# Six of sixteen token tiles transposed by VectorE through DRAM instead of by TensorE

## The chip, the cores and the metric

The kernel runs on one core of one Trainium2 chip. The metric is the time of one execution on the device in microseconds (us). Before the change three runs took 562.86, 564.63 and 564.69 us, so the median is 564.63 us.

## The reference

The input `x` is 2048 tokens of 512 features in float32. It is normalised once, and two branches use the result: a linear attention with 32 heads of 16 features, and a gated feed-forward network with 1376 hidden features. Their outputs are multiplied and added to `x`:

```python
xn = layernorm(x)                                  # no scale, no shift, eps 1e-5
q, k, v = split(xn @ wqkv)                         # 32 heads of 16
pq, pk = q @ w_phi, k @ w_phi                      # per head, 16x16
phi_q = concat(softmax(pq), softmax(-pq))
phi_k = concat(softmax(pk), softmax(-pk))
kv, z = phi_k^T @ v, sum(phi_k)
s = ((phi_q @ kv) / (phi_q @ z + 1e-6)) @ wo
g = silu((relu(xn @ W_gate) * (xn @ W_up)) @ W_down)
out = x + s * g
```

## The kernel before, in words

**Precision.** Each float32 operand of a large matmul is split into a rounded high part and the low remainder (`split`, L193: ScalarE writes the high part, VectorE or GpSimd subtracts to get the low part). `mm3` (L198) then makes three matmuls of each product.

**Tiles and stages.** The 2048 tokens are 16 tiles of 128 tokens, in four blocks of four tiles. `order` (L219) alternates between two blocks: tiles 0 to 7 take turns between blocks 2 and 3, tiles 8 to 15 between blocks 0 and 1. So tiles 2m and 2m+1 lie at the same place of two blocks.

Stage one is the loop over n at L1046, one token tile a turn. TensorE (PE in the profile) makes `pk` and `pv`, the key and value projections of tile n (12 matmuls each), and `pq`, a piece of the query projection (`query`, L364, 12 matmuls), and adds `pkv`, the key-value products of an earlier tile (`kv_products`, 8 matmuls). `query(n-1)` reads the transposed tiles of a group of four: in turn 9 `query(8)` reads tiles 8 to 11, and in turn 13 `query(12)` reads tiles 12 to 15. The vector engines make the softmax features of `pk` (`exponents`, `features`). GpSimd (POOL) splits the features and issues a DMA that adds them into the sum `zacc` (`features_split`, L429).

Stage two, from about 167 us, goes twice over 11 slices of the hidden features (`gate_up`, `down`), half of the tokens each time. It uses a 2x2 block product with seven products in place of eight, so the sums and differences S1 to S4 of the transposed tokens are wanted too. Beside it the queries' features are made on VectorE, ScalarE and GpSimd (`all_queries`, L1172). Each half ends with the output tiles (`pso`).

**The transposed tokens.** `XT` (L255) holds, for each token column, eight pieces in high and low parts: A21, A22 of the odd tile, A11, A12 of the even one, and S1 to S4. For tile m these steps make it:

- `load_x(m)`: a DMA from `x` on the queue of SyncE (SP).
- `norm_stats`, `norm_scale`, `norm_apply` (L259 to L276): ScalarE (ACT) makes mean and variance with two passes whose written output is not used (they go to the buffer `xn`), VectorE (DVE) and GpSimd make the scale, and ScalarE writes the normalised tile into `xn`.
- `turn(m)` (L320): four PE transposes of 128x128 into one PSUM bank `pxT`; ScalarE copies it to the high part of `XT` (`hi_xt`) and again to a full-precision buffer `xf` (`full_xt`); VectorE writes the low part (`lo_xt`) from `pxT`.
- `sums_x(m)` for odd m: GpSimd makes S1 to S4 from the two `xf` tiles with four operations into two new buffers `sa` and `sb`; `sums_hi` and `sums_lo` split them into `XT`.

In turn n the loop loads tile n+7, scales tile n+5, applies the norm to tile n+4, transposes tile n+3 between `pk` and `pv` (LEAD is 3, L30), and makes the statistics of tile n+6.

**What sets the order.** The program is written out by a planner, `Clock` (L62). Every engine runs its instructions in program order, and work that isn't urgent (weight preparation `f_prep`, the queries, the stores) is written as generators. `pump` lets a generator go on when the planner's estimate of the engines' time says that its inputs are ready; a DMA counts as landed 8000 PE cycles after its issue, with a margin of 3000 more before another step may use it. A generator that yields a number waits that many times 512 PE cycles. `finish` runs a generator to its end at once.

**Buffers.** Tiles of a tag share slots: 41 of 2 KB a partition (`u2`), 8 of 4 KB (`u4`: the features `ek`, the value parts `vhl`, raw weights), 8 PSUM banks of which `pkv` holds four through stage one. A new tile waits until an old one of its tag is let go.

Of the kernel before, what the change touches and what calls it, by code (L numbers as in the profile page):

```python
# [1 line left out]

# [11 lines left out]
P = 128  # L14
# [15 lines left out]
LEAD = 3  # L30
QUERIES = [(0, 1, 2), (6, 7, 4, 5, 3)]
# [10 lines left out]
A21, A22, A11, A12, S1, S2, S3, S4 = range(8)  # L42
# [19 lines left out]
class Clock:  # L62
# [7 lines left out]
    shared = None  # L70
# [13 lines left out]
    def issued(self, key, name, a, k):  # L84
        o, ins = a[0], [*a[1:], *k.values()]
        n = max(x.free_size() for x in [o, *ins] if hasattr(x, "free_size"))
        start = max([self.now, *(self.there(x) + 200 for x in ins)])
        if name == "dma_start":
            self.ready[o.name] = start + self.LANDING
            if key == "gpsimd":  # L90
                self.free[key] = max(start, self.free[key]) + self.ISSUE
            return
        cost = self.RATE[key] * n
        if key == "tensor":
            n = o.free_size()
# [6 lines left out]
        self.ready[o.name] = self.free[key] + (380 if key == "tensor" else 0)  # L102

# [55 lines left out]
def layer_kernel(ctx: ExitStack, tc: tile.TileContext, x, wkT, wqT, wv, wo, wf, cst, out):  # L159
# [15 lines left out]
    def u2(shape, name, dt=F32):  # L175
        return sb.tile(list(shape), dt, tag="u2", bufs=B2, name=name)
# [7 lines left out]
    def f32(t):  # L184
        return t.bitcast(F32)
# [68 lines left out]
    mhalf = sb.tile([P, 96], F32, name="mhalf")[:, 0:1]  # L254
    XT = sb.tile([P, 8, 2, 2, BT], F32R, tag="XT", name="XT")  # L255
    pace.shared = XT.name
    XN, XF, SF = {}, {}, {}

    def norm_stats(n):  # L259
        xt = X.pop(n)  # L260
        xn = u2((P, D), "xn")
        sm, ss, rs, bias = small(1, "lm"), small(1, "lv"), small(1, "lr"), small(1, "lb")
        nc.scalar.activation(xn, xt, AF.Copy, scale=-1.0 / D, accum_out=sm)
        nc.scalar.activation(xn, xt, AF.Square, bias=sm, accum_out=ss)
        XN[n] = xn, xt, bias, rs, sm, ss

    def norm_scale(n):
        xn, xt, bias, rs, sm, ss = XN[n]
        nc.vector.tensor_scalar(rs, ss, 1.0 / D, 1e-5, op0=ALU.mult, op1=ALU.add)
        nc.gpsimd.tensor_tensor(rs, rs, mhalf, op=ALU.pow)  # L270

    def norm_apply(n):
        xn, xt, bias, rs, sm, ss = XN[n]
        nc.vector.tensor_scalar(bias, sm, rs, None, op0=ALU.mult)
        nc.scalar.activation(xn, xt, AF.Identity, bias=bias, scale=rs)
        XN[n] = xn  # L276
# [32 lines left out]

    def hi_xt(n, p):  # L310
        nc.scalar.activation(xt_part(n, 0), p, AF.Copy)
# [5 lines left out]
    def lo_xt(n, p):  # L317
        add(nc.vector, xt_part(n, 1), p, f32(xt_part(n, 0)), ALU.subtract)
# [8 lines left out]
    def sums_x(n):  # L327

        x0, x1 = XF.pop(n - 1), XF.pop(n)
        sa, sb_ = u2((P, 2, 2, P), "sa"), u2((P, 2, 2, P), "sb")  # L330
        add(nc.gpsimd, sa[:, 0], x1[:, 0], x1[:, 1])
        add(nc.gpsimd, sb_[:, 0], x0[:, 0], x1[:, 0], ALU.subtract)
        add(nc.gpsimd, sa[:, 1], sa[:, 0], x0[:, 0], ALU.subtract)
        add(nc.gpsimd, sb_[:, 1], x0[:, 1], sa[:, 1], ALU.subtract)
        SF[n] = sa, sb_

    def sums_hi(n):
        for s, c in zip(SF[n], (S1, S3)):
            nc.scalar.activation(XT[:, c:c + 2, 0, :, cols(n)], s, AF.Copy)

    def sums_lo(n):
        for s, c in zip(SF.pop(n), (S1, S3)):
            add(nc.gpsimd, XT[:, c:c + 2, 1, :, cols(n)], s, f32(XT[:, c:c + 2, 0, :, cols(n)]), ALU.subtract)
# [112 lines left out]
    def f_load(f):  # L456
        if f == AHEAD[-1]:

            t = u4((P, 2, 2, 2, P), "rawg")
            RAW[f] = [t[:, c] for c in range(2)], u2((P, D), "rawd")  # L460
            nc.sync.dma_start(t.rearrange("p c k s f -> p (c k s f)"), wf[f][:, :1024])
        else:
            RAW[f] = two("rawg", f not in AHEAD), u2((P, D), "rawd")
            for c in range(2):
                nc.sync.dma_start(RAW[f][0][c].rearrange("p k s f -> p (k s f)"), wf[f][:, c * 512:(c + 1) * 512])
        nc.sync.dma_start(RAW[f][1], wf[f][:, 1024:])
# [520 lines left out]
    nc.sync.dma_start(wq_raw[:, 2:4, :], wqT[:, 2:4, :])  # L987
# [39 lines left out]

    def all_preps():
# [16 lines left out]
    at = [0]  # L1045
    for n in range(N):  # L1046
        at[0] = n
        if n + 7 < N:
            load_x(n + 7)
        if n == 2:  # L1050
            preps = pace.add(all_preps(), 0, 3)
        if 1 < n < N - 4:
            norm_apply(n + 4)
        if 0 < n < N - 5:
            norm_scale(n + 5)
# [5 lines left out]
        turned = [turn(n + LEAD)] if 1 < n < N - LEAD else [turn(3)] if n == 1 else []  # L1061
# [271 lines left out]
```

## Time and profile before

| What | Value |
|---|---|
| median of three runs | 564.63 us |
| the profiled execution, its time | 562.9 us |
| its span, first to last instruction | 561.1 us |
| PE busy | 556.3 us, 99% |
| DVE, ACT, POOL busy | 412.0, 282.7, 416.2 us |
| granted PE clock | 0.999 |
| DMA moved | 137.98 MB, mean 246 GB/s |
| PE transposes | 64, between 6.0 and 129.1 us |

The span is 1.8 us shorter than the execution's time. A row of the groups gives the engine, the operation, the output and inputs by name, their shape, the count, the busy time and mean duration, and the idle time that the engine spent just before these instructions. Matmul durations overlap (each is pipelined into the next), so the pace of PE is read from start to start, or from the pieces of the chain, which stand end to end. Nearly every instruction is issued through one helper, so line numbers say L58 throughout and the tiles' names tell the operations apart.

### The profile page before, as it was taken

Reading aid. Unit: us, or ns where it says so; the run is one execution under the profiler, and the core shown is the slowest. Engines: PE = TensorE matmul, PEld = TensorE weight load, DVE = VectorE, ACT = ScalarE, POOL = GpSimd, SP = SyncE. Lnnn points to the kernel's source line nnn. Section 1 sums busy time; section 2 is a strip of 40 time slices with the busy share of each in tenths; the row PEclk is TensorE's granted clock in tenths of the full one; section 3 lists DMA queues with packets and bytes.
Section 4 is the critical chain, followed back from the end, with each engine's and each line's share of the span. In section 5 each row is a group of like instructions: output and inputs, shape, how many; then the busy total and the mean of one; then the engine's idle time right before and its main releaser. Section 6 shows DMA issues by size and latency. Waiting matters only on the chain.

```text
span 561.1 us, 8204 instructions
## 1 busy us (share of the span) xinstructions
PE 556.3 (99%) x2618; PEld 466.0 (83%) x2618; DVE 412.0 (73%) x623; ACT 282.7 (50%) x504; POOL 416.2 (74%) x356
## 2 busy tenths in 40 slices
PE   9999999999999999999999999999999999999997
PEld 8888888888888888888888888888888888888886
DVE  5978777677656898999798432699995959775324
ACT  3898687765545456444425251234463544534500
POOL 1689987898888386998889242572879788888474
PEclk9999999999999999999999999999999999999999
DMA  8349999765599827979767899997475666659675
GB/s 282 136 150 245 274 277 330 213 167 166 150 297 314 327 77 276 326 270 324 263 240 230 246 356 419 401 374 282 137 225 178 219 204 206 207 166 284 170 237 193
DMA packets 84538, 137.98 MB, mean 246 GB/s; under 512 B 7824, under 2 KB 34320, under 8 KB 83600
## 3 DMA queue, kind: packets, MB, share of 16 engines
q1 hardware_dynamic: 81040, 125.33, 65.1%
q0 software_dynamic: 3312, 12.06, 11.0%
q8 instruction: 21, 0.34, 0.3%
q14 instruction: 21, 0.17, 0.1%
q10 hardware_dynamic: 144, 0.07, 0.0%
HBM read 76.87 MB, written 52.69 MB: 231 GB/s over the span
## 4 chain that ended last, share of the span: by engine, by line
PE 99%; DVE 0%; issue 0%
PE py L58 21%; PE pc L58 11%; PE pa L58 11%; PE pd L58 11%; PE pv L58 8%; PE pk L58 8%; PE pq L58 8%; PE pso L58 8%; PE pb L58 5%; PE pkv L58 3%; PE pnum L58 3%; PE pxT L58 1%; PE pfold L58 1%; PE pidle L58 1%; PE pz L58 0%; DVE yk L58 0%
## 5 line engine op out<-in xcount | busy, mean ns | idle before, releaser
L58 PE MATMUL py<-fdh,hl 128*128 128x512 f32 x176 | 68.5, 389 | 0.0
L58 PE MATMUL py<-fdh,hh 128*128 128x512 f32 x176 | 68.5, 389 | 0.0
L58 PE MATMUL py<-fdl,hh 128*128 128x512 f32 x176 | 68.5, 389 | 0.0
L58 PE MATMUL pa<-XT,wa 128*128 128x512 f32 x264 | 67.4, 389 | 0.0
L58 POOL TENSOR_TENSOR hl<-e,hh 128x512 fp32r<-128x512 f32 x22 | 28.5, 1296 | 44.9 <-ACT hh L58 40.0
L58 PEld LDWEIGHTS pa<-XT,wa 128*128 128x128 f32 x264 | 49.5, 188 | 10.2
L58 ACT ACTIVATE hh<-e 128x512 fp32r<-128x512 f32 x22 | 13.9, 633 | 72.5 <-DVE e L58 70.1
L58 DVE TENSOR_TENSOR y<-py,y 128x512 f32<-128x512 f32 x40 | 27.5, 689 | 24.7 <-PE py L58 24.7
L58 POOL TENSOR_TENSOR phl<-ek,phl 128x1024 fp32r<-128x1024 f32 x15 | 36.1, 2409 | 11.1 <-ACT phl L58 11.1
L58 PE MATMUL pv<-wvh,XT 128*128 128x512 f32 x128 | 43.5, 401 | 0.0
L58 PE MATMUL pk<-wkh,XT 128*128 128x512 f32 x128 | 42.4, 392 | 0.0
L58 POOL TENSOR_TENSOR hl<-u,hh 128x512 fp32r<-128x512 f32 x22 | 28.8, 1311 | 16.6 <-ACT hh L58 14.3
L58 POOL TENSOR_TENSOR ez<-eq,zB 128x1024 f32<-128x1024 f32 x16 | 38.5, 2411 | 3.3 <-ACT eq L58 2.7
L58 PE MATMUL pq<-XT,wqh 128*128 128x512 f32 (+1 forms) x144 | 40.3, 366 | 0.0
L58 PEld LDWEIGHTS py<-fdh,hl 128*128 128x128 f32 x176 | 33.0, 188 | 6.9
L58 PEld LDWEIGHTS py<-fdh,hh 128*128 128x128 f32 x176 | 33.0, 188 | 6.8
L58 PEld LDWEIGHTS py<-fdl,hh 128*128 128x128 f32 x176 | 33.0, 188 | 6.8
L58 POOL TENSOR_TENSOR ol<-of,oh 128x512 fp32r<-128x512 f32 (+1 forms) x13 | 19.9, 1551 | 23.3 <-ACT oh L58 15.9
L58 PE MATMUL pc<-XT,wc 128*128 128x512 f32 x132 | 34.9, 392 | 0.0
L58 PE MATMUL pd<-XT,wc 128*128 128x512 f32 x132 | 33.8, 389 | 0.0
L58 PE MATMUL pc<-XT,wb 128*128 128x512 f32 x132 | 33.7, 389 | 0.0
L58 PE MATMUL pd<-XT,wd 128*128 128x512 f32 x132 | 33.5, 389 | 0.0
(162 smaller groups left out, 1581.0 us busy)
## 6 DMA issues: line engine op xcount, KB each, us to landing
zacc<-ek POOLq DMA_DIRECT2D x15, 512.0 KB, 6.0
xts<-XT SPq DMA_DIRECT2D x4, 1792.0 KB, 8.8
XT<-xts SPq DMA_DIRECT2D x7, 1024.0 KB, 19.6
wa<-ws SPq DMA_DIRECT2D x26, 256.0 KB, 5.0
wb<-ws SPq DMA_DIRECT2D x26, 256.0 KB, 4.4
wc<-ws SPq DMA_DIRECT2D x26, 256.0 KB, 5.0
ws<-wa SPq DMA_DIRECT2D x22, 256.0 KB, 4.5
ws<-wb SPq DMA_DIRECT2D x22, 256.0 KB, 4.2
```

Source lines behind the costliest of these rows:

```text
L58: return self.tc.keep_in_program_order(op(*a, **k))
```

## The change: what it does

Tiles 10 to 15 (`BLOCKWISE = 10` and up) no longer go through `turn`. For them:

- `norm_stats` writes its unused outputs to a PSUM bank (`unread`); `xn` is taken later, in `norm_apply`, which writes the tile with the features in an order `(a k i)` in place of `(k a i)`, where i counts 32 features, a four groups and k four chunks.
- A generator `by_blocks` stores `xn` to DRAM (256 KB), waits, loads it back with four DMAs of 64 KB, one for each group of 32 partitions, so that 32-token pieces stand in the rows where they belong, and then lets VectorE transpose 32x32 blocks, 128x512 in one instruction. Its output `xf` is in the SBUF, with the tokens' blocks of 32 as an own axis. `hi_xt`, `lo_xt` and `sums_x` read it there; `full_xt` falls away.
- The main loop makes sure at the end of odd turns n that tiles n+1 and n+2 are done.

For all tiles, `sums_x` now writes its four results in the place of `xf` instead of into `sa` and `sb`; the order of S1 and S3 in `XT` is changed so that each pair written together lies together. Other parts: from turn 5 on tile n+8 is loaded, from turn 6 on statistics are made for n+7, from 7 on the scale for n+6, from 8 on the norm is applied to n+5. The last two pieces of `wq` and the gate/up weights of slice 3 are loaded with two DMAs in place of one. The queries of the first half no longer pause for 24 times 512 PE cycles after `state`.

```diff
+BLOCKWISE = 10
+LAND = (12, 12)
-A21, A22, A11, A12, S1, S2, S3, S4 = range(8)
+A21, A22, A11, A12, S3, S1, S2, S4 = range(8)
...
     def norm_stats(n):
         xt = X.pop(n)
-        xn = u2((P, D), "xn")
+        xn = None if n >= BLOCKWISE else u2((P, D), "xn")
+        unread = xn or ps(name="unread")
...
     def norm_apply(n):
+        xn = xn or u2((P, D), "xn")
+        if n < BLOCKWISE:
+            nc.scalar.activation(xn, xt, AF.Identity, bias=bias, scale=rs)
+            XN[n] = xn
+        else:
+            nc.scalar.activation(xn.rearrange("p (a k i) -> p k a i", a=4, i=32),
+                                 xt.rearrange("p (k a i) -> p k a i", a=4, i=32), AF.Identity, bias=bias, scale=rs)
+            TURN[n] = pace.add(by_blocks(n, xn), 0, 3, True)
+
+    def by_blocks(n, xn):
+        xd = dram((P, D), f"xn{n}")
+        yield "sync", xn
+        nc.sync.dma_start(xd, xn)
+        yield LAND[0],
+        yield "sync", xd
+        t = u2((P, 4, P), "xp")
+        for a in range(4):
+            r = slice(32 * a, 32 * a + 32)
+            nc.sync.dma_start(t[r], xd.rearrange("(b q) (a c) -> a q b c", q=32, a=4)[a])
+        yield LAND[1],
+        yield "sync", t
+        while at[0] < n - LEAD:
+            yield 1,
+        yield "vector", t
+        o = u2((P, D), "xf")
+        nc.vector.transpose(o, t.rearrange("p b c -> p (b c)"))
+        XF[n] = o.rearrange("p (b c k q) -> p c k b q", b=4, c=2, k=2)
+        yield "scalar", o
+        hi_xt(n, XF[n])
+        yield "vector", pace.mark("scalar")
+        lo_xt(n, XF[n])
+        if n % 2:
+            yield "gpsimd", o
+            sums_x(n)
...
     def sums_x(n):
         x0, x1 = XF.pop(n - 1), XF.pop(n)
-        sa, sb_ = u2((P, 2, 2, P), "sa"), u2((P, 2, 2, P), "sb")
-        add(nc.gpsimd, sa[:, 0], x1[:, 0], x1[:, 1])
-        add(nc.gpsimd, sb_[:, 0], x0[:, 0], x1[:, 0], ALU.subtract)
-        add(nc.gpsimd, sa[:, 1], sa[:, 0], x0[:, 0], ALU.subtract)
-        add(nc.gpsimd, sb_[:, 1], x0[:, 1], sa[:, 1], ALU.subtract)
-        SF[n] = sa, sb_
+        add(nc.gpsimd, x1[:, 1], x1[:, 0], x1[:, 1])
+        add(nc.gpsimd, x1[:, 0], x0[:, 0], x1[:, 0], ALU.subtract)
+        add(nc.gpsimd, x0[:, 0], x1[:, 1], x0[:, 0], ALU.subtract)
+        add(nc.gpsimd, x0[:, 1], x0[:, 1], x0[:, 0], ALU.subtract)
+        SF[n] = x1, x0
...
     for n in range(N):
         at[0] = n
-        if n + 7 < N:
-            load_x(n + 7)
+        up_to(n + 7 + (n > 4), load_x)
...
+        if n > 1:
+            up_to(n + 4 + (n > 7), norm_apply)
+        if n:
+            up_to(n + 5 + (n > 6), norm_scale)
...
-        turned = [turn(n + LEAD)] if 1 < n < N - LEAD else [turn(3)] if n == 1 else []
+        m = n + LEAD
+        if 1 < n < N - LEAD and m >= BLOCKWISE:
+            turned = []
+        else:
+            turned = [turn(m)] if 1 < n < N - LEAD else [turn(3)] if n == 1 else []
...
-        if n + 6 < N:
-            norm_stats(n + 6)
+        up_to(n + 6 + (n > 5), norm_stats)
         if n % 2 and n + 2 < N:
+            for m in (n + 1, n + 2):
+                if m in TURN:
+                    pace.finish(TURN.pop(m))
             sums_hi(n + 2)
...
             yield from state()
-            yield 24,
```

`up_to(m, op)` calls `op` for every tile up to m that hasn't had it.

More of the change, by code (lines that the diff above doesn't have):

```diff
@@ L1 @@
 from contextlib import ExitStack
+from types import SimpleNamespace
 import concourse.bass as bass
@@ L456, in f_load @@
     def f_load(f):
[L457 to L465, printed above, removed]
+        RAW[f] = two("rawg", f not in AHEAD), u2((P, D), "rawd")
+        for c in range(2):
+            nc.sync.dma_start(RAW[f][0][c].rearrange("p k s f -> p (k s f)"), wf[f][:, c * 512:(c + 1) * 512])
         nc.sync.dma_start(RAW[f][1], wf[f][:, 1024:])
```

52 lines of the change are left out of this document (30 added, 22 removed).

## The prediction

> **What bounds the kernel now.** I read the page's busy shares first, then the chain that ended last, then PE's own waits, and then the chain piece by piece around the turns that change.
>
> ```profile
> PE 556.3 (99%) x2618; PEld 466.0 (83%) x2618; DVE 412.0 (73%) x623; ACT 282.7 (50%) x504; POOL 416.2 (74%) x356
> ...
> PEclk9999999999999999999999999999999999999999
> ...
> PE 99%; DVE 0%; issue 0%
> ...
> PE pidle L58 <- DVE mhalf L58: 1.1, 1, 1.1
> ```
>
> The chain is PE from end to end, its only wait in the whole span is 1.1 us at the start, and its clock is full throughout. So only what PE executes, and any new wait of PE, moves the end. In the pieces of the chain (start, length, what) the turns stand one behind the other:
>
> ```profile
> 78.19 2.75 PE pk L58 x12
> 80.94 0.44 PE pxT L58 x4
> ...
> 87.81 2.75 PE pk L58 x12
> ...
> 97.44 2.75 PE pk L58 x12
> ...
> 103.38 2.72 PE pq L58 x12
> 106.10 2.72 PE pk L58 x12
> ...
> 115.69 2.72 PE pk L58 x12
> ...
> 125.27 2.72 PE pk L58 x12
> ...
> 134.86 2.72 PE pk L58 x12
> ...
> 144.00 2.72 PE pk L58 x12
> ```
>
> Each `pk` begins a turn. Turns 7 and 8 take 9.62 and 9.63 us, turn 9 takes 8.66 (it has no `pkv`), turns 10 to 12 take 9.59, 9.58 and 9.59. Turn 13, the first with no transposes, takes 9.14.
>
> **PE: what is removed.** Tiles 10 to 15 were transposed in turns 7 to 12: 24 of 64 transposes go. By difference: turns 7 and 8 save 0.48 and 0.49 against 9.14; turn 9 saves 0.50 against its three projections (3 x 2.72 = 8.16); turns 10 to 12 save 0.45, 0.44 and 0.45. The sum is 2.8 us. The lower bound is the six `pxT` pieces alone, 6 x 0.44 = 2.6; the upper is 6 x 0.50 = 3.0. I take 2.8, as it holds the handover to `pv` too.
>
> ```profile
> L58 PE MATMUL pxT<-ident,xn 128*128 128x128 f32 x64 | 9.9, 282 | 0.0
> ...
> L58 DVE STREAM_TRANSPOSE ez<-eq 128x512 f32<-128x512 f32 x16 | 10.7, 691 | 0.0
> ...
> L58 ACT ACTIVATE xf<-pxT 128x512 f32<-128x512 f32 x16 | 9.4, 588 | 0.0
> ...
> L58 DVE TENSOR_TENSOR XT<-pxT,XT 128x512 fp32r<-128x512 f32 x16 | 11.0, 690 | 6.9 <-ACT xf L58 5.4 <-ACT XT L58 1.5
> ...
> L58 DVE TENSOR_TENSOR yk<-yk,sx 128x512 f32<-128x512 f32 x1 | 1.3, 1254 | 0.0
> ...
> L58 POOL TENSOR_TENSOR sa<-xf 128x256 f32<-128x256 f32 x8 | 7.4, 926 | 0.2 <-ACT xf L58 0.2
> ```
>
> The 282 ns in the first row is not the price of a transpose: four take 0.44 us in the chain, 0.11 each. The Trainium skill (VectorE: DVE Perf Modes, The three transpose paths and Rules for kernel authors) says to use TensorE for a 128x128 transpose if PSUM will do as its destination, and puts one at 390 ns; by that figure 24 would save about 9.4 us, an estimate from that page, and the time would be near 555. By that figure the trace disagrees: its 0.11 us holds. Its advice against leaving TensorE has no cost in this trace either, since DVE is not in the chain.
>
> **DVE.** Six transposes of 128x512 are added: 6 x 0.69 = 4.1 us. Six low parts now have two SBUF inputs in place of PSUM and SBUF: between 0.69 and 1.25 each (the `yk` row, the nearest with two SBUF inputs), at most 3.4 more. Both lie beside PE as long as DVE has room:
>
> ```profile
> core 0: us, PE busy (x) PEld busy (x) DVE busy (x) ACT busy (x) POOL busy (x), PEclk, DMA share, GB/s
> ...
> 78.00:88.00 10.00, 10.00 (x52) 8.45 (x51) 7.47 (x12) 6.72 (x14) 9.74 (x11) 1.00 1.11 325
> 88.00:97.50 9.50, 9.50 (x49) 7.98 (x48) 8.22 (x14) 7.33 (x15) 6.58 (x6) 1.00 1.08 318
> 97.50:106.00 8.50, 8.50 (x41) 7.02 (x40) 5.59 (x10) 6.04 (x13) 8.42 (x12) 1.00 0.83 214
> 106.00:115.70 9.70, 9.70 (x50) 8.26 (x49) 6.42 (x12) 8.79 (x17) 8.07 (x9) 1.00 0.51 165
> 115.70:125.30 9.60, 9.60 (x49) 8.16 (x49) 8.04 (x12) 5.49 (x9) 9.52 (x10) 1.00 0.74 202
> 125.30:134.90 9.60, 9.60 (x49) 8.15 (x49) 6.73 (x10) 5.40 (x10) 9.12 (x9) 1.00 0.80 209
> ```
>
> DVE is idle at least 1.3 us in each stretch, a tile adds at most 1.25: zero on the path. Without that cover DVE's 4.1 to 7.5 us would be late for `pk`'s and `pv`'s readers.
>
> **ACT.** Six `xf` copies of 0.59 go, 3.5 us less. The high parts read SBUF instead of PSUM and the norm writes in pieces of 32; I cost both at nothing, between the same passes' present price and 0.1 us more each, as ACT is idle 0.9 us or more in every stretch above. The two statistics passes write to a PSUM bank: it takes a bank at turns 4 to 8, three turns or more before the one that `pxT` no longer takes. Turns 4 to 6 so want one bank more each (turn 6 two). Bounds: 0 to 0.6 us of PE in each of three turns (one pass of ACT before a bank is let go); I take 0, since PE waits for no bank now.
>
> **POOL.** The same four sums a pair, 0.93 us for the one shown, written in place; they now wait for DVE's transpose where they waited for `xf`. Nothing is added. Two buffers a pair are let go earlier.
>
> **SP and the DMA queues.** Six stores and 24 loads are added: 30 issues at some 0.33 us.
>
> ```profile
> 81.64 0.80 ACT L58 ACTIVATE xn<-xt,lb,lr 128x512 f32<-128x512 f32 x1
> ...
> L58 SPq DMA_DIRECT2D xt<-x x16: 327/352/7489, 0.7 to 85.7; - x16
> L58 ACT ACTIVATE xn<-xt x12: 615/631/667, 21.0 to 108.3; 128x512 f32<-128x512 f32 x12
> ...
> DMA to landing us min/median/max: 2.8/7.3/10.7
> ...
> ws<-wa SPq DMA_DIRECT2D x22, 256.0 KB, 4.5
> ...
> SPq L58 <- ACT pqs L58: 36.4, 10, 7.3
> ```
>
> These are a row of the timeline, three of the tile `xt` (durations are min/median/max in ns, then the first and last start), one of the DMA view and one of SP's waits. 30 x 0.33 is 10 us of SP spread over seven turns, while SP waits 36.4 us for `pqs` alone. Behind a load that waits for its store stand the next `xt` loads, the query spills and the weight stores. The `xt` load issued last, at 85.7, is read at 108.3, so it can be late by some 12 us. All of that costs 0.
>
> The tightest place is tile 11, which `query(8)` reads in turn 9. Its norm ends at 82.4. The planner counts 542 cycles for a matmul that takes 2.72 / 12 = 0.227 us in the chain, so its 3000 cycles before the store are 1.3 us (83.7), and the 12 x 512 + 8000 + 3000 between store and loads 7.2 us (90.9, or later if the store hasn't landed). With a landing of 7.3 us each, the median of `xt` (same size, same turns), the data is there at 98.3, and transpose, high and low part (0.69 + 0.6 + 0.7 to 1.25) end at 100.3 to 100.9. `query(8)` starts at 103.4 less two turns' saving, 102.4: 1.5 us or more to spare. Bounds: at 4.5 us (the `ws` row) the planner's second 7.2 us holds the transpose to 98.1, and 1.7 us are to spare; at 10.7 twice it is late by 5.3. I take 0.
>
> **The other edits.** The split of the `wq` and slice-3 loads adds two issues; PE waits for neither now: 0 (bounds -0.4 to 0.4, an issue each way). Loading, statistics and norms one tile earlier move ACT and SP work by a turn: 0. The new order of S1 to S4 moves addresses only: 0. Dropping the pause of 24 starts the first half's queries some 5 us sooner.
>
> ```profile
> 182.00:196.00 14.00, 14.00 (x63) 11.59 (x63) 11.76 (x19) 5.83 (x15) 5.97 (x4) 1.00 0.89 335
> 196.00:210.00 14.00, 14.00 (x64) 11.59 (x63) 13.83 (x20) 7.43 (x14) 11.12 (x11) 1.00 0.21 79
> ```
>
> DVE is full from 196 (13.83 of 14) and PE has no wait even then. Earlier by 5 us fills 182 to 196, where 2.2 us of DVE are free: 0, bounds 0 to 3 us (5 less the 2.2 free), taken at the cover that the rows show.
>
> **The sum.** 2.8 us less PE, all else beside it. The profiled execution took 562.9 us, 1.7 under the median of the runs shown; it would take 560.1. On the median, 564.63 - 2.8 = 561.8 us.
>
> **The rivals.**
>
> *Slower: the DMA engines fall behind, and features wait for buffers.* By 103 us the change adds both transfers of tiles 10 and 11 and the stores of 12 and 13: 6 x 0.262 = 1.57 MB, where the DMA share is already 0.83 to 1.11 from 78 on.
>
> ```profile
> 85.91 0.60 ACT L58 ACTIVATE vhl<-pv 128x512 fp32r<-128x512 f32 x1 [1.98 <-DMA zacc<-ek]
> ...
> 94.00 0.60 ACT L58 ACTIVATE vhl<-pv 128x512 fp32r<-128x512 f32 x1 [0.51 <-DMA zacc<-ek]
> ...
> 102.78 0.69 DVE L58 TENSOR_TENSOR ek<-pk,mx 128x512 f32<-128x512 f32 x1 [1.26 <-DMA zacc<-ek]
> ```
>
> For: buffers of the features are let go by the `zacc` DMA, and three times an engine already waits for it. At 320 GB/s the added bytes are 4.9 us of backlog. `pk` of turn 9 is let go at 104.1 (the row at 102.78 and one more subtraction), the next `pk` starts at 106.1: 2.0 us to spare. If each of the three waits grew by the backlog, PE would lose 3 x 2.9 = 8.7 us: 570.5. It decides when more than 5.6 us reaches PE. Against: `zacc` has a queue of its own, and turns without `pxT` hold a bank less. Chance 0.19.
>
> *Tile 11 is late.* The DMA view of 40 to 75 us has
>
> ```profile
> xt<-x SPq DMA_DIRECT2D x4, 256.0 KB, 10.2
> ```
>
> At 10.2 us for both landings the tile would be ready at 106.4 and PE would wait 4.0 at `query(8)`: 565.8; at the bound of 5.3, 567.1. It decides from a landing of some 8 us twice. Against: the median of 7.3. Chance 0.16.
>
> *The change doesn't do what it says: POOL holds the turn.* POOL is busy 9.52 of 9.60 in turn 11 and 9.12 in turn 12, so a turn of 9.14 leaves it no room. If each of the six new low parts shuts POOL out for its 1.25 us, POOL loses 7.5 us; two of them fall before 97.5, where it is idle 3.2 us from 78 on, and four (5.0 us) between 97.5 and 134.9, where it is idle 2.3. The 2.7 us left over would pass to PE and eat the gain: 564.6 - 2.8 + 2.7 = 564.5. The Trainium skill states that lock (SBUF — State Buffer, SBUF: two separate sides: a DVE operation with two SBUF inputs and a GpSimd operation that reads SBUF shut each other out); the trace agrees so far as the `yk` row's 1254 ns stands against 690. Against: POOL's share holds weight preparation that can be put off. Chance 0.09.
>
> **How the numbers follow.** The forecast, full saving, has 0.56. A measurement of this kernel can't tell less than about 0.5%, 2.8 us, from no change, so the forecast lies on that bound. The median of the runs shown stands at their upper end (562.86 to 564.69); a draw from their middle, 563.8, less 2.8 gives 561.0, so I put 6 in 10 of this case beyond the bound: 0.34 faster. The other 0.22, the late tile (0.16) and POOL (0.09) end within the bound: 0.47. The backlog alone is slower: 0.19. Range: from the lowest run less 2.8, 560.0, to 567.5, which takes in the late tile and POOL and leaves out the backlog; the forecast's own is 560.0 to 562.8.
>
> **What would show it.** Right: 40 transposes in place of 64 on PE, turns 7 to 12 of 9.14 us (8.16 in turn 9), PE with no wait but the first, the end of stage one 2.8 us sooner. Wrong: a PE wait before `pq` of turn 9 on `XT`; longer waits of `vhl` or `ek` for `zacc`, and PE waiting for a PSUM bank behind them; POOL without idle time to 135 us; or a PE wait after 182 us, which would point to the pause.

## The result, and the profile after

| | before | after |
|---|---|---|
| median of the runs | 563.64 us (8 runs, 562.48 to 564.69) | 568.46 us (8 runs, 566.01 to 570.23) |
| profiled execution, and its span | 562.9, 561.1 us | 567.09, 565.3 us |
| TensorE transposes of tokens | 64 | 40 |

The ratio is 1.0083, with a 95% interval of 1.0058 to 1.0108. The change makes the kernel 0.8% slower, and the forecast of 561.8 us, with its range to 567.5, missed it.

Two lines of the page of the kernel after: busy shares, and the chain that ended last.

```profile
PE 555.4 (98%) x2594; PEld 462.8 (82%) x2594; DVE 421.6 (75%) x629; ACT 279.3 (49%) x498; POOL 417.4 (74%) x356
...
PE 68%; POOL 11%; DMA 9%; DVE 4%; ACT 3%; issue 3%; SPq 1%; POOLq 0%; ACTq 0%
```

TensorE was 99% of the chain and is 68% of it now. POOL's busy time has grown by 1.2 us, VectorE's by 9.6, of which six transposes explain 4.2.

The chain itself, kernel after, in order of time (start, length, what), between 89 and 139 us:

```profile
89.81 5.51 DMA xn<-xn
...
96.92 3.74 DMA xp<-xn
...
100.68 0.71 DVE xf L63
101.39 3.60 DVE XT L63 x2
...
123.18 4.16 DVE XT L63 x3
...
135.70 2.47 DVE XT L63
138.17 0.66 DVE mx L63 x2
```

This is tile 11's whole way: its store, its loads, VectorE's transpose, and then two low parts (`XT`, those of tiles 10 and 11) in 3.60 us, where 0.69 to 1.25 each was expected. Three more of them take 4.16 us, and one alone 2.47.

The timeline of the kernel after (start, duration, engine, instruction; in brackets the idle time ahead of it and what ended it). First the rows of TensorE ahead of and behind each new gap, with the first `pa` (the start of the second stage) and the first `py`:

```profile
71.61 0.65 PE L63 MATMUL pxT<-ident,xn 128*128 128x128 f32 x4
73.05 0.50 PE L63 MATMUL pv<-wvh,XT 128*128 128x512 f32 x1 [0.80 <-ACT unread L63]
...
103.35 0.39 PE L63 MATMUL pq<-XT,wql 128*128 128x512 f32 x1
...
105.05 0.73 PE L63 MATMUL pq<-XT,wqh 128*128 128x512 f32 x2 [1.31 <-DVE XT L63]
...
125.51 0.61 PE L63 MATMUL pq<-XT,wqh 128*128 128x512 f32 x2
126.36 0.47 PE L63 MATMUL pk<-wkh,XT 128*128 128x512 f32 x1 [0.23 <-DVE XT L63]
...
138.32 1.11 PE L63 MATMUL pkv<-phl,vhl 128*128 128x256 f32 x8
...
140.71 0.47 PE L63 MATMUL pv<-wvh,XT 128*128 128x512 f32 x1 [1.28 <-DVE ek L63]
...
169.19 1.07 PE L63 MATMUL pa<-XT,wa 128*128 128x512 f32 x4
...
179.69 1.52 PE L63 MATMUL pa<-XT,wa 128*128 128x512 f32 x6
...
182.40 1.67 PE L63 MATMUL pb<-XT,wb 128*128 128x512 f32 x6 [1.19 <-POOL wb L63]
...
189.37 0.84 PE L63 MATMUL pd<-XT,wd 128*128 128x512 f32 x3
190.45 0.50 PE L63 MATMUL pz<-zl,ones 128*128 128x512 f32 x1 [0.24 <-POOL zl L63]
...
196.25 0.39 PE L63 MATMUL py<-fdh,hl 128*128 128x512 f32 x1
```

and the same two marks, with ACT's copies that will matter below, in the timeline of the kernel before:

```profile
165.15 0.62 ACT L58 ACTIVATE wb<-tab 128x512 fp32r<-128x512 f32 x1
...
166.78 1.52 PE L58 MATMUL pa<-XT,wa 128*128 128x512 f32 x6
...
174.45 1.06 ACT L58 ACTIVATE zh<-zacc 128x1024 fp32r<-128x1024 f32 x1 [1.27 <-DMA zacc<-ek]
...
191.78 0.39 PE L58 MATMUL py<-fdh,hl 128*128 128x512 f32 x1
```

The first stage ends 2.41 us later (169.19 against 166.78) though 24 transposes are gone, and by the first `py` it is 4.47. What a gap costs is the distance between the starts around it less the ordinary pitch (0.227 us for 512 columns, 0.12 for `pkv`, 0.11 for `pxT`):

| at | who waits | cost |
|---|---|---|
| 72 us | `pv`, for the PSUM bank of the unread statistics | 73.05 - 71.61 - 4 x 0.11 = 1.0 |
| 103 | `pq` of `query(8)`, for a low part | 105.05 - 103.35 - 0.23 = 1.5 |
| 126 | `pk`, for a low part | 126.36 - 125.51 - 2 x 0.23 = 0.4 |
| 139 | `pv`, for `ek`, behind a low part on VectorE | 140.71 - 138.32 - 8 x 0.12 = 1.4 |
| 181 | `pb`, for slice 1's weights | 182.40 - 179.69 - 6 x 0.23 = 1.3 |
| 190 | `pz`, for the low part of z | 190.45 - 189.37 - 3 x 0.23 = 0.4 |

That is 6.0 us. The matmul behind each wait adds 0.1 (six times, 0.6), and the first three turns begin 0.46 us later, a difference that other profiles of kernels with this start show as 0.1 to 0.9 (`e_lock` below, which starts as the kernel before does, shows 0.2). Less 2.7 us for 24 transposes at 0.11 this makes 4.4, and 4.47 were measured. So every row of the loss has a place; the experiments are about the causes. (The medians differ by 4.8 us; the profiled execution of the kernel after was one of its faster ones, at a granted clock of 1.000, where two of its eight runs had 0.996 and took 569.7 and 570.2 us.)

Three more readings of the same timeline give them. Two of POOL's feature splits beside low parts; then the table that slice 1's weights are made from (`tab`), and what stands in ACT's queue ahead of them:

```profile
101.32 3.68 DVE L63 TENSOR_TENSOR XT<-xf,XT 128x512 fp32r<-128x512 f32 x2
...
101.62 2.83 POOL L63 TENSOR_TENSOR phl<-ek,phl 128x1024 fp32r<-128x1024 f32 x1
...
135.22 2.40 POOL L63 TENSOR_TENSOR phl<-ek,phl 128x1024 fp32r<-128x1024 f32 x1 [4.41 <-ACT phl L63]
...
135.70 2.47 DVE L63 TENSOR_TENSOR XT<-xf,XT 128x512 fp32r<-128x512 f32 x1 [1.08 <-ACT XT L63]
...
175.97 1.56 POOL L63 TENSOR_TENSOR tab<-rawg,tab 128x256 f32<-128x256 f32 x2
...
179.41 1.06 ACT L63 ACTIVATE zh<-zacc 128x1024 fp32r<-128x1024 f32 x1 [2.74 <-DMA zacc<-ek]
180.38 0.62 ACT L63 ACTIVATE wb<-tab 128x512 fp32r<-128x512 f32 x1
...
181.07 1.27 POOL L63 TENSOR_TENSOR wb<-tab,wb 128x512 fp32r<-128x512 f32 x1 [2.15 <-ACT wb L63]
```

The split of POOL ends at 104.45 and 137.62; the low parts end at 105.00 and 138.17, both 0.55 us later. In the kernel before the low part reads PSUM, and all 16 last 0.68 to 0.69 us whatever POOL does. That gives theory A: a low part with two SBUF inputs stands still until POOL's instruction beside it has ended. Its rivals: B, the tile is simply late by way of DRAM; C, the rest comes from late weight preparation; D, from the other edits. For the weights the rows say where they stand: `tab` is done at 177.53, but ACT waits for `zacc` from 176.67 on and copies `wb` only behind `zh`, at 180.38.

### The profile page after: what moved, and what is told of

Its sections match the earlier page's. It is cut to its first block, busy times and chain, and to the rows that moved or that the text cites. A ratio compares the mean times of both kernels' runs of the same rounds, so it can differ in the third digit from the quotient of the medians.

```text
span 565.3 us, 8205 instructions
## 1 busy us (share of the span) xinstructions
PE 555.4 (98%) x2594; PEld 462.8 (82%) x2594; DVE 421.6 (75%) x629; ACT 279.3 (49%) x498; POOL 417.4 (74%) x356
## 4 chain that ended last, share of the span: by engine, by line
PE 68%; POOL 11%; DMA 9%; DVE 4%; ACT 3%; issue 3%; SPq 1%; POOLq 0%; ACTq 0%
PE py L63 21%; PE pc L63 10%; PE pd L63 10%; PE pa L63 10%; PE pso L63 8%; PE pb L63 5%; DMA zacc<-ek 3%; PE pnum L63 3%; POOL phl L63 2%; POOL XT L63 2%; DVE XT L63 2%; DMA xn<-xn 2%; DMA wvr<-wv 2%; POOL xf L63 1%; DMA xp<-xn 1%
## 5 line engine op out<-in xcount | busy, mean ns | idle before, releaser
L63 PE MATMUL pb<-XT,wb 128*128 128x512 f32 x132 | 33.6, 390 | 1.2 <-POOL wb L63 1.2
```

Of the source, the lines that this page charges most:

```text
L63: return self.tc.keep_in_program_order(op(*a, **k))
```

## The experiments

### The low part alone, and the other edits alone

`e_lock`: the kernel before, but the low parts of tiles 10 to 15 read the SBUF copy.

```diff
+        if n >= 10:
+            p = FULL.pop(n)          # the xf copy of the same tile
         add(nc.vector, xt_part(n, 1), p, f32(xt_part(n, 0)), ALU.subtract)
```

> The kernel before, in its own order, with one operand changed: for tiles 10 to 15 the low part is made from the full-precision copy in the SBUF instead of from the PSUM bank (everything else, the PE transposes too, stays). Theory A (a DVE operation with two SBUF inputs waits until the GpSimd instruction that is reading the SBUF is through): the six low parts last from 0.69 up to about 2.9 us where they meet GpSimd's 2.4 us split of the features, and PE gets new waits: 564.5 to 567 against 563.6. Theory B (the cause lies in the DMA traffic): no DMA is added here, so the low parts last 0.69 to 1.25 us, and the time stays at 563.6.

Measured: 563.07 us, ratio 0.9991 (0.9978 to 1.0004). The time doesn't move, but the low parts do: they last 0.69, 1.33, 0.68, 1.02, 2.70 and 1.88 us. The longest, in the timeline of that kernel:

```profile
122.64 2.41 POOL L58 TENSOR_TENSOR phl<-ek,phl 128x1024 fp32r<-128x1024 f32 x1
122.89 2.70 DVE L58 TENSOR_TENSOR XT<-xf,XT 128x512 fp32r<-128x512 f32 x1 [0.35 <-ACT xf L58]
```

It ends 0.54 us behind the split, as in the kernel after. So the standstill is there without DRAM and without VectorE's transposes, but here nobody waits for it: the tile's products come turns later and VectorE's idle time covers the rest.

`e_other`: every edit but the transposes by VectorE.

```diff
-BLOCKWISE = 10
+BLOCKWISE = 16
```

> The changed kernel with no tile transposed in blocks (all 16 by PE), so that only the other edits are left: sums in place, looks one tile further ahead, the two split loads, no pause before the queries. If the loss comes from the transposes through DRAM: 563.6 within 0.5 us, no PE wait over 0.5 us. If the other edits carry a part of it (the PE wait of 1.3 us for weights at 181 us and of 0.4 us at 190 us are theirs): 564.5 to 566.

Measured: 565.62 us, ratio 1.0036 (1.0024 to 1.0048), so the other edits alone cost 2.0 us. Its profile has none of the gaps of the kernel after from 100 us on: the first `pa` comes 1.1 us late and the last matmul 1.5, of which 0.9 belong to the first three turns; then 1.3 more pass behind the last matmul, 0.7 of them because the last output's issue stands in SP's queue behind those of `y` (1.9 us behind the start of the last matmul, 1.2 in the kernel after). That tail is not in the kernel after (565.3 - 561.5 = 3.8 us behind the last matmul, 4.0 before), so these 2.0 us can't be carried over as a sum. Nor does TensorE wait behind 182 us here, though the pause is dropped in this run too.

`e_unread`: the statistics' unread output goes to SBUF.

```diff
-        unread = xn or ps(name="unread")
+        unread = xn or u2((P, D), "unread")
```

> The changed kernel in its own order; the statistics' unused output goes to an SBUF buffer instead of a PSUM bank. If the bank is what pv waits for at 72 us: that PE wait (1.0 us) goes and the time falls from 568.5 by about 1 us, to 567.5. If PE waits there for ScalarE's lateness itself, the wait passes to another bank and the time stays at 568.5.

Measured: 568.34 us, ratio 1.0087 (1.0065 to 1.0109). The wait at 72 us is gone, so the bank was its cause, and the next one takes a part of the gain: `pq` waits 2.0 us for the low part in turn 9 instead of 1.3, as TensorE comes there sooner than the low part can follow. The order on the four engines is that of the kernel after, and at the first `py` this profile is 1.25 us ahead (195.00). It loses that at the end, though: 0.6 us at 555, where `pso` waits for `ol`, and 1.3 more behind the last matmul. So the wait is shown, and what its removal is worth by itself is not.

### Taking the standstill away

`e_low_psum`: all six tiles get a second VectorE transpose into PSUM, which the low part reads.

```diff
         nc.vector.transpose(o, t.rearrange("p b c -> p (b c)"))
+        p = ps(name="pxB")
+        nc.vector.transpose(p, t.rearrange("p b c -> p (b c)"))   # not in the planner's account
...
-        lo_xt(n, XF[n])
+        lo_xt(n, p)                  # in the block order of XF[n]
```

> The changed kernel in its own order; VectorE makes the 32x32 transpose a second time, into a PSUM bank (0.7 us more of VectorE a tile), and the low part reads that bank. Theory A (two SBUF inputs wait for GpSimd): the low parts fall back to 0.69 us, PE's waits at 103, 126 and 139 us (3.4 us in the profile of the changed kernel) go or shrink to under 1 us, and the time falls from 568.5 to 565 to 566. Theory B (DMA traffic makes the tiles late): nothing is gained, 568.5 or more.

Measured: 570.79 us, ratio 1.0134 (1.0110 to 1.0159). The low parts last 0.69 us each (two in 1.26), and the gaps at 103 and 139 us are gone, as theory A has it. But a new one of 5.2 us opens, in the timeline of that kernel:

```profile
113.28 0.71 DVE L63 STREAM_TRANSPOSE xf<-xp 128x512 f32<-128x512 f32 x1 [3.23 <-DMA xp<-xn]
...
117.46 0.67 DVE L63 TENSOR_TENSOR ek<-mx,pk 128x512 f32<-128x512 f32 x1
...
118.28 0.76 PE L63 MATMUL pq<-XT,wql 128*128 128x512 f32 x1 [5.22 <-DVE ek L63]
```

VectorE waits 3.23 us for tile 12's data, issues four transposes, and only then the features of `pk` (`mx`, `ek`), for which `pq` waits. Here theory B is right about the wait at the head of VectorE's queue: in this kernel, with one bank and two instructions more for the two tiles, it reaches TensorE. Whether the bank or the instructions bring it there, the run doesn't say.

`e_low_odd`: the same for tiles 11 and 15 alone.

```diff
+        if n in (11, 15):
+            p = ps(name="pxB")
+            nc.vector.transpose(p, t.rearrange("p b c -> p (b c)"))
```

> The changed kernel, with one thing added: tiles 11 and 15 alone are transposed a second time by VectorE into a PSUM bank, and their low parts read that copy. Theory A (the low part with two SBUF inputs stands still behind POOL's split, and TensorE waits behind it twice): the low parts of tiles 11 and 15 last 0.69 us instead of 2.87 and 2.47, the 1.31 us wait of pq near 103 us and the 1.28 us wait of pv near 140 us fall below 0.4 us, and the weights' wait near 181 us stays or grows by up to 1.5 us: 564.5 to 567.5 us. Theory B (the tile comes late by way of DRAM, POOL has no part in it): both waits stay above 1.0 us, and the two more transposes add up to 1.4 us: 568 to 570 us.

Measured: 566.93 us, ratio 1.0060 (1.0042 to 1.0078), in the band of A, but that is luck, as the steps are others. Tile 11's low part lasts 0.68 us, and `pq` waits 1.3 us all the same: tile 10's low part, ahead of it, still reads SBUF, meets the split and lasts 2.67. Whichever part comes first stands. The gap at 139 us is gone, as A has it for tile 15, and `pv` waits 2.0 us near 130 us for the bank that `pqs` reads instead. In this profile (567.83 us) the first `pa` comes 1.7 us later than in the kernel after, and `pb` waits 0.2 us for its weights instead of 1.2.

`e_split4`: no bank, no other order; POOL's split is issued in four pieces.

```diff
-        split(phl[:, :, 0, :], phl[:, :, 1, :], src, nc.gpsimd)
+        nc.scalar.activation(phl[:, :, 0, :], src, AF.Copy)
+        for g in range(0, NG, 2):    # from turn 7 on; one instruction in the planner's account
+            r = slice(g, g + 2)
+            nc.gpsimd.tensor_tensor(phl[:, r, 1, :], src[:, r, :], f32(phl[:, r, 0, :]), op=ALU.subtract)
```

> The changed kernel with the order of TensorE and VectorE as it is; from turn 7 on only POOL's split of the features (phl, 128x1024, 2.40 us) is issued as four instructions of 128x256 (0.7 to 1.0 us each, 3 to 4 us together). Theory A (a low part with two SBUF inputs stands until the POOL instruction that runs beside it has ended): it now stands one piece instead of the whole, so the low parts last at most 1.7 us instead of 2.87, 2.51 and 2.47; the waits of pq near 103 us (1.31) and of pv near 140 us (1.28) fall to 0.5 us or less each; the weights' wait near 181 us stays, as POOL works a little more: 565.5 to 567.5 us. Theory B (the tile's way by way of DRAM is what is late): low parts and waits as they were, and POOL's longer split makes it 568 to 570 us.

Measured: 564.23 us, ratio 1.0017 (1.0004 to 1.0030): 4.2 us under the kernel after by the medians and 3.7 by the ratios (beside this run the kernel before took 562.98 us), more than A asked for. Rows of its timeline, and its waits of TensorE (total, times, longest):

```profile
101.29 2.29 DVE L63 TENSOR_TENSOR XT<-xf,XT 128x512 fp32r<-128x512 f32 x2
...
101.84 3.73 POOL L495 TENSOR_TENSOR phl<-ek,phl 128x256 fp32r<-128x256 f32 x4
...
133.37 0.81 DVE L63 TENSOR_TENSOR XT<-xf,XT 128x512 fp32r<-128x512 f32 x1 [1.09 <-ACT XT L63]
...
165.78 1.52 PE L63 MATMUL pa<-XT,wa 128*128 128x512 f32 x6
...
192.95 0.39 PE L63 MATMUL py<-fdh,hl 128*128 128x512 f32 x1
```

```profile
PE pb L63 <- POOL wb L63: 1.2, 1, 1.2
...
PE pv L63 <- ACT unread L63: 0.8, 1, 0.8
PE pz L63 <- POOL zl L63: 0.3, 1, 0.3
PE pq L63 <- DVE XT L63: 0.2, 1, 0.2
```

POOL works longer, and VectorE and TensorE come sooner: the low parts get in between two pieces. The first stage now ends at 165.78, 1.0 us before the kernel before and 3.4 before the kernel after. Of the 3.4 us, 0.35 are an earlier start; the low parts' three gaps have gone from 3.6 us (with the matmul behind each) to 0.5. The order of the instructions is that of the kernel after on all four engines; only POOL's splits stand in four pieces. So theory A is shown: 3.1 us of the profile, where the times themselves say 3.7 to 4.2. B can't be the cause of those, as the way through DRAM is the same. What is left, the bank at 72 us and the weights at 181, stands in the waits with the prices that it had.

### The late weights

`e_preps`: the tiles' generators stand behind the weight preparation in the planner's list.

```diff
-            TURN[n] = pace.add(by_blocks(n, xn), 0, 3, True)
+            TURN[n] = pace.add(by_blocks(n, xn), 0, 3)
```

> The changed kernel, but the generators of the six tiles stand behind the weight preparation in the planner's list instead of ahead of it. Theory C (the tiles' generators have pushed the weight preparation of the first two slices about 15 us later, and TensorE waits for it at 181 and 190 us): the table of slice 0 is made before 150 us instead of at 158, the wait of pb for wb near 181 us (1.19 us) and that of pz for zl are gone, while the waits near 103 and 140 us stay or grow: 565.5 to 567.5 us. If the preparation isn't what is late there, the time stays at 568 us or above.

Measured: 566.57 us, ratio 1.0051 (1.0036 to 1.0067). The gaps at 103 and 181 us are gone; that at 139 has grown to 1.8 us, and the other order brings waits of 0.8 us at 165 (`pkv` for `phl`) and 0.7 at 373 (for a reload). That of `pz` for `zl`, which was to go too, has grown from 0.2 to 0.5 us. `wb` is now copied at 171.03, ahead of `zh`: it was the tiles' generators, put ahead of the preparation, that made it late.

`e_early`: one number.

```diff
         f_load(0)
-        yield 30,
+        yield 14,
```

> The changed kernel with one number changed: after the load of slice 0's raw weights its preparation pauses 14 matmuls' time instead of 30, so that it starts some 8 us earlier. Theory C (late weights cost 2.1 us at 177 to 190 us): pb no longer waits for wb, and the time falls by 1.5 to 2.1 us, to 566.3 to 567 us; the waits near 103 and 140 us stay. If POOL's earlier preparation only moves the low parts or the features' split later, the time stays within 0.5 us of the changed kernel's 568.4.

Measured: 565.09 us, ratio 1.0034 (1.0021 to 1.0047): 3.4 us under the kernel after by the medians, 2.8 by the ratios, and below the band of C. Rows in the timeline of this kernel:

```profile
169.19 1.07 PE L63 MATMUL pa<-XT,wa 128*128 128x512 f32 x4
...
174.94 0.63 ACT L63 ACTIVATE wb<-tab 128x512 fp32r<-128x512 f32 x1 [3.59 <-POOL tab L63]
...
179.59 1.06 ACT L63 ACTIVATE zh<-zacc 128x1024 fp32r<-128x1024 f32 x1 [2.93 <-DMA zacc<-ek]
...
194.22 0.39 PE L63 MATMUL py<-fdh,hl 128*128 128x512 f32 x1
```

That the first `pa` stands at 169.19 as in the kernel after is chance: the wait at 105 us is 1.0 us instead of 1.3, and that at 126 is gone, but the first turns begin later. From there to the first `py` it takes 25.03 us, with no wait of TensorE, where the kernel after takes 27.06 and the kernel before 25.00. So late preparation costs 2.0 us in the profile; the times say 2.8 to 3.4, with about 1 us of uncertainty on either. One number moves more than the weights, though: the planner also issues the products for `z`, and with them other work, in another order.

`e_next`: on top of the split in four, the load of slice 1's raw weights four steps earlier.

```diff
         put(f, 5, wc[1])
+        if keep and f == 0:
+            f_load(1)
...
-            if nxt < NF:
+            if 0 < f and nxt < NF:
                 f_load(nxt)
```

> The split of the features in four, and the load of slice 1's raw weights issued four steps earlier in slice 0's preparation; the order on TensorE, VectorE, ACT and POOL is that of the split alone. If ACT's and POOL's start on slice 1 waits for that load (ACT waited 2.85 us for it in the changed kernel), wb comes 1 to 2 us earlier, the waits of TensorE near 177 and 186 us fall from 1.9 us to under 0.8, and the time from 564.2 to 562.8 to 563.5 us. If POOL's own queue is what is late, 564.2 us stays.

Measured: 565.46 us, ratio 1.0040 (1.0025 to 1.0055); no gain. Its timeline says why:

```profile
176.32 1.06 ACT L63 ACTIVATE zh<-zacc 128x1024 fp32r<-128x1024 f32 x1 [4.34 <-DMA zacc<-ek]
177.28 0.61 ACT L63 ACTIVATE wb<-tab 128x512 fp32r<-128x512 f32 x1
```

With the data there, ACT stands 4.34 us instead of the 2.82 of `e_split4` ahead of `zh`, which waits for the last features' accumulate into `zacc`, and `wb` stands behind it. Neither of the two causes offered was it: the weights aren't late by their load nor by POOL, but by their place in ACT's queue. In the kernel before `wb` is copied at 165.15, 9 us ahead of `zh`; in the kernel after it comes behind. The other profiles bear this out: whenever `wb` comes ahead of `zh`, TensorE doesn't wait for it.

`e_pause`: the pause of 24 put back.

```diff
             yield from state()
+            yield 24,
```

> The changed kernel with the pause of 24 before the first query blocks put back, as the kernel before has it. If dropping the pause costs time (the two products for z wait for the low part of z, and ahead of them the weights of slice 1 are late), the waits of pz near 190 us (0.2 us, with 0.4 us lost) are gone: 567.5 to 568.2 us, and at most 1 us less. If the pause does nothing here: 568.5 us, within 0.7.

Measured: 585.62 us, ratio 1.0393 (1.0367 to 1.0419). Neither expectation had this. The first stage's longer gaps and the wait for `wb` (1.4 us) are there as in the kernel after. The first `pnum` comes at 238.4 instead of 222.1, and of the four groups of it that are done by 271 us in the kernel after, two are done by 249 and two come at 293 and 300. The sixteen matmuls that stood at 306 to 315 come at 326 to 335, and TensorE waits 11.9 us for them in four places; the granted clock is 0.50 from 326 to 336. The longest row:

```profile
325.66 0.58 PE L63 MATMUL pnum<-pTh,XT 128*128 128x256 f32 x1 [9.32 <-ACT pTh L63]
```

So the pause is no small matter in this order. `z` comes 10 us later than before (190.45 against 180.68), and the pause brings the first `pnum` another 16 us; that the two together are what makes the queries too late is argued from these times, and no run tests it.

### Four tiles, and the causes together

`e_blk12`, `e_blk12u`, `e_b12e`, `e_blk12s`: tiles 12 to 15 alone by VectorE; then with the statistics in SBUF; then with the earlier preparation as well; and, the last, with statistics in SBUF, generators behind the preparation, and the split in four.

```diff
-BLOCKWISE = 10
+BLOCKWISE = 12
```

> The changed kernel with four tiles by VectorE (12 to 15) instead of six; 10 and 11 by TensorE. The theory that the query products of turn 9 wait for tile 11's low part: the 1.31 us wait near 103 us is gone; two tiles give 0.9 us of TensorE's transposes back; the wait near 140 us for tile 15's low part stays; the wait for the unread statistics' bank moves to a later turn or goes: 566 to 568 us. If only the number of tiles counted, a third of the loss would go: 566.8 us.

> Four tiles by VectorE (12 to 15), and their unread statistics go to SBUF instead of a PSUM bank. If that bank is what pk waited for near 79 us in the run with four tiles (2.2 us behind pqs on ACT), that wait is gone and the time falls by about 2.2 us, to 564.5 to 566.5 us; if it is another bank's turn, the wait stays or moves to another place and the time is that of the run with four tiles, 567 to 569 us.

> Four tiles by VectorE, unread statistics in SBUF, and the earlier preparation; POOL's split whole. The run without the earlier preparation took 565.0 us and had 1.7 us of waits at 178 to 187 us: 563.0 to 563.8 us if they go, no different from the kernel before. If the preparation displaces POOL's other work: 565 us or more.

> Four tiles by VectorE, the unread statistics in SBUF, the tiles' generators behind the weight preparation, and POOL's split of the features in four pieces from turn 7 on: every cause found so far is taken away. Saved are 16 transposes, 16 x 0.11 = 1.8 us. If the causes are complete: 561.5 to 563 us, at or under the kernel before (563.3). If a wait takes their place, 564 to 567 us, and the profile shows which.

Measured: 568.02 us, 1.0089 (1.0059 to 1.0119); 565.01, 1.0037 (1.0021 to 1.0054); 564.00, 1.0023 (1.0007 to 1.0039); and 568.08, 1.0088 (1.0059 to 1.0117). With four tiles the wait near 103 us is gone, and against the expectation that near 140 as well, but `pk` waits 2.2 us near 79 for the bank that `pqs` reads; with the statistics out of PSUM that wait is gone and the time falls by 3.0 us, so there the bank was the cause. Two low parts last 5.86 us in that run, and TensorE waits 0.3 us for `ek` behind them: the standstill is only as dear as what stands behind it. The earlier preparation saves 1.0 us more where 1.2 to 2.0 were expected, as `pv` then waits 2.1 us for `ek` near 119. The last run misses by the order that its edits cause: a low part starts at 119.4 us beside POOL's weight preparation and lasts 9.4 us, through nine POOL instructions in a row, four of them pieces of a split, and `pk` waits 4.4 us for it; the granted clock is 0.50 behind that wait, from 129 to 133. Pieces help only where VectorE gets in between them.

`e_combo` (tiles 11 and 15 as in `e_low_odd`, statistics in SBUF, generators behind the preparation), `e_se` (split in four and earlier preparation), `e_seu` (that and the statistics in SBUF), `e_nextu` (`e_next` and the statistics in SBUF):

> The changed kernel with three edits together: the second transpose into PSUM for the low parts of tiles 11 and 15, the unread statistics in SBUF instead of a PSUM bank, and the tiles' generators behind the weight preparation. If these three causes are all of the loss (3.3 us of low parts behind POOL, 1.0 us of the bank, 2.0 us of late weights), 568.5 - 6.3 = 562.2 us, from 561 to 563.5, at or below the kernel before. If a wait takes their place again, 565 to 568 us, and the profile shows which.

> The split of the features in four and the earlier preparation together. If both causes are separate and the list is complete but for the bank: 564.2 - 2.1 = 562.1 us (561.5 to 562.8), under the kernel before by 0.9. If the earlier preparation takes POOL's time where the low parts stand: 563.5 to 565 us.

> As the run before, and the unread statistics in SBUF instead of a PSUM bank (1.0 us lost near 72 us): 561.1 us (560.5 to 562.3) if all the losses are named, which is 563.0 less the 2.7 us of the 24 transposes plus the start's 0.4 to 0.5. If the freed bank moves the wait elsewhere, as it did when it was taken away alone: 562 to 564 us.

> As e_next, and the unread statistics in SBUF: the wait of 0.8 us near 72 us goes, and the time is 1.0 us under that of e_next: 561.8 to 562.6 us, under the kernel before (563.1) by 0.5 to 1.3. If the freed wait comes back behind another buffer: as e_next, within 0.5 us.

Measured: 565.46 us, 1.0041 (1.0027 to 1.0055); 563.50, 1.0009 (0.9998 to 1.0020); 564.27, 1.0023 (1.0006 to 1.0039); 566.04, 1.0048 (1.0031 to 1.0064). `e_se` is the best of all with tiles by VectorE, 4 to 5 us under the kernel after and not to be told from the kernel before. The causes don't add up to a gain: each order that takes one wait away has others. In `e_se` these are 0.4 and 0.5 us for low parts, 0.7 for `e` on VectorE at 177 and still 0.8 for the bank; in `e_seu`, without the bank, `e` takes 1.7, and nothing is gained; in `e_combo` 1.3 for `ek` at 119, behind transposes for which VectorE waited 6.0 us; in `e_nextu` 2.2 for `wb`. No kernel with tiles by VectorE came below the kernel before.

## Why the prediction was wrong

- **TensorE's 2.8 us: right.** 40 transposes are left, and where no wait lies the turns are as short as said: `e_split4` reaches the end of the first stage 1.0 us sooner than the kernel before, with 1.0 and 0.5 us of waits and 0.1 us of start in it: 1.0 + 1.6 = 2.6. The 390 ns that the prediction gives from the Trainium skill (VectorE: DVE Perf Modes, The three transpose paths) stand there for bf16 and these transposes are float32; the forecast went by the trace's 0.11 us, and that held.
- **DVE: this step failed first.** "Between 0.69 and 1.25 each" for a low part with two SBUF inputs, and "a tile adds at most 1.25: zero on the path". They last up to 2.87, 2.51 and 2.47 us, and TensorE waits behind them. The `yk` row was no upper bound: its 1254 ns was already an instruction that stood beside POOL, by as much as that neighbour happened to last (`yk` ended 0.55 us behind POOL's `y`). Even the longest POOL instruction and 0.55 us, some 3 us, would have been too little as a bound: `e_blk12s` has 9.4.
- **The third rival had the mechanism and the wrong victim.** It let the low part hold POOL, and cited the Trainium skill (SBUF — State Buffer, SBUF: two separate sides) for a lock between the two. The same section says that whichever instruction starts first keeps it to its end while the other waits. By that sentence the trace agrees: POOL's split started first and VectorE waited (2.47 us, ending 0.55 behind the split). One instruction is no bound for the wait, though: in `e_blk12s` VectorE stood through nine of POOL's, and there the measurement decides. Of the rule's two directions only the cheap one was worked out (564.5 us), where the dear one costs 3.6 us of TensorE.
- **Tile 11: half right.** The data was forecast for 98.3 us and landed at 100.7: its store was issued at 89.8 and not at 83.7, as tile 10's four loads, two spills and three weight loads stood ahead of it in SP's queue, and the two transfers then took 5.5 and 5.3 us instead of 7.3 each. With low parts of 0.69 us that would nearly have been in time, as `e_split4` shows, whose two low parts there last 1.14 and 1.23 us (0.2 us of wait at 103 us). Late tile and standstill together used up the 1.5 us.
- **ACT, the bank: mis-sized in one place.** "0 to 0.6 us of PE in each of three turns", taken as 0: it is 1.0 us in one turn, at 72 us, in turn 6, the one that wants two banks more. Taken away alone, it leaves the median where it was (`e_unread`).
- **"The other edits", each 0: wrong.** By themselves they cost 2.0 us (`e_other`), a part of it at the start and at the end. The step on the pause (0, bounds 0 to 3) looked at VectorE's room, and `e_other` has no wait there; in the order of the kernel after, putting the pause back costs 17 us. A wait after 182 us was to "point to the pause"; one came at 182.4, and it pointed to ACT's queue, where slice 1's weights stand behind `zh`. The forecast had no step for the order of weight preparation, and that cost 2.0 us.
- **The first rival, the DMA engines, wasn't it.** `zacc` lands as before (median 5.8 us, 6.0 before). In the first stage `vhl` waits 2.8 us for it in all, 2.5 before, and `ek`'s 1.3 us are gone; only `zh`'s wait in the second has grown, from 1.3 to 2.7.

In short: saved 2.7; lost 3.6 to low parts behind POOL, 2.0 to weights behind `zh`, 1.0 to a bank, 0.5 at the start. Of the 3.6, `e_split4` takes 3.1 away; the 2.0 are shown by `e_early` with `e_next` and the rows of ACT. Of the bank the wait is shown (`e_unread`), but its price only with four tiles, where it was another wait of 2.2 us. The 0.5 us at the start stays open: the same start showed 0.1 to 0.9 in other profiles, and no run split it further.

## What to carry to other kernels

When an operand moves from PSUM to SBUF, the instruction's price is no longer its own: bound it by the instructions of the engine that it may have to wait for, by several of them where they follow each other closely, and ask what stands behind it in its queue. A long instruction can be issued in pieces so that others get in between; here that was worth 3 to 4 us without moving any other instruction, where VectorE got in between the pieces. And where a planner orders the work, an edit's price includes the order that it causes: look at what each engine does first behind a DMA wait.

## What the runs showed of the hardware that was not expected

- A VectorE subtraction of 128x512 with two SBUF inputs, 0.69 us with one of them in PSUM, lasts until 0.55 us behind POOL's work beside it: 2.47, 2.70 and 2.87 us beside one instruction of 2.40 to 2.83. Between two POOL instructions it sometimes gets in (in `e_split4` the low part that starts at 102.35 ends 0.55 us behind the first of four pieces, and the pieces beside low parts last 1.18 and 1.19 us instead of 0.74) and sometimes not: 4.16 us through three in a row in `e_blk12u`, 9.36 through nine in `e_blk12s`. POOL's records overlap by 0.2 to 0.6 us where VectorE stands on, one gap with a DMA issue in it excepted, and by 0.05 or less, or not at all, where it gets in; which of the two follows from the other stays open. VectorE's transposes from SBUF, with one input, stayed at 0.67 to 0.72 us beside the same work.
- TensorE's clock fell behind a wait. The rows of two stretches of `e_low_psum` (length, busy time of PE, PEld, DVE, ACT, POOL, then the granted clock):

```profile
112.50:118.20 5.70, 0.56 (x3) 0.13 (x1) 4.86 (x8) 1.89 (x4) 5.70 (x5) 0.83 1.03 307
118.20:123.20 5.00, 4.92 (x12) 3.80 (x12) 4.41 (x6) 1.31 (x3) 0.49 (x1) 0.51 0.67 187
```

  Behind 5.2 us of waiting the clock was 0.51 for 5.0 us, about 2.5 us more of loss, which is in that run's time. So it was behind the 4.4 us of `e_blk12s` (0.50 for 4 us). The Trainium skill (TensorE: Matmul & The Clock Gate, Part 1: The HAM clock gate) puts the fall behind an idle window of some 3.4 us; by that, these rows agree. In `e_low_odd`, though, a wait of 2.0 us at 129 was followed by a clock of 0.63 from 134 to 137, while it was 1.00 from 180.3 to 196 behind the 2.2 us wait of `e_nextu`.
